# Local attention and a squared-ReLU layer: the first block as two groups of 256 tokens, a hand-fixed issue order, weights converted 1024 columns at a time, s r^2 kept in PSUM

## The chip, the cores and the metric

The kernel runs on one core of one Trainium2 chip. TensorE (PE) multiplies matrices and writes PSUM; VectorE (DVE), ScalarE (ACT) and GpSimd (POOL) do the elementwise work; SyncE (SP) issues the DMAs that bring data from HBM to SBUF. PEld is TensorE's loading of weights, which runs beside its matmuls. The metric is the device time of one execution in microseconds; lower is better. A profiled execution has a span, from its first to its last instruction, and a time, which is a little longer.

## The reference, cut to what matters

```python
# q, k, v: (8 batch, 8 heads, 576 positions, 64), float32; chunks of 64 positions
scores = 1/8 * q_c @ k_c^T                    # inside one chunk only
attn = exp(scores - max) / (sum + 1e-9)
x = (attn @ v_c), heads side by side          # 4608 tokens x 512
h = x @ w_in                                  # w_in: 512 x 2048, given in float64
g = s * relu(h)**2 + b                        # s, b: one number each
out = g @ w_out                               # w_out: 2048 x 512, given in float64
```

## The kernel before

**Blocks.** 4608 tokens are nine blocks of 512. For each block the layer runs over 16 slices j of 128 hidden columns. `up(j)` makes h for the slice: 12 matmuls into one bank of PSUM (`ps_h`, two buffers), because every float32 operand is carried as a high and a low part (fp32r) and three of the four products are summed, over four pieces of 128 rows. Then ScalarE takes the ReLU into `r` (L176), VectorE makes s r^2 in place in `r` (L177), ScalarE adds b and rounds to the high part `gh` (L179), VectorE makes the low part `gl` (L180). `down(j)` adds the slice's product to four accumulators (`ps_o`, L193, 12 matmuls); it runs two slices behind `up`. `store` copies the accumulators to SBUF (L199) and sends them off (L200).

**Attention** of the next block is laid between these steps. In the steady blocks a group has 256 tokens, two groups to a block: `s_scores` (64 matmuls of 64x64, L115, then maximum, subtraction, exponential, sum, normalisation, L118 to L128), `s_pt` (8 transposes L136, copies L137), `s_pv` (64 matmuls L143, then `split` into `xh` and `xl`, L57 and L58). The first block has no block before it and is done in four groups of 128 tokens, before the layer starts.

**Weights** come as float64, two 32-bit words to a number, and stay in SBUF after the first block. There are 32 pieces of 128x512, two for each j: (j, 0) for `up`, (j, 1) for `down`. A piece is loaded into `raw` (L66, 512 KB), and `narrow` and `split` turn it into high and low float32: ScalarE scales both words (L75, L76), VectorE shifts and joins bits (L78, L79), GpSimd adds the tail (L81), ScalarE copies the high part (L57), VectorE subtracts for the low part (L58). Each of these works on 512 columns. `next_weights` does one step of this between two steps of the layer, all through the first block.

**Order.** The code gives the instructions in an order of dependence and priority; a scheduler of the framework, which works with estimated durations, sets the order on each engine's queue from it. In a few places `issue_after` keeps an instruction behind another. All DMAs go through the SP queue, s and b as well, third and fourth in it.

**Buffers.** `raw` has four buffers of 4 KB a partition, for weights and for the queries and keys of later blocks; `rawv` two; the attention tiles `p`, `m`, `z`, `pT` one each; `ps_a`, two banks, one; `ps_o` two of two banks.

Of the kernel before, what the change touches and what calls it, by code (L numbers as in the profile page):

```python
# [8 lines left out]
F32 = mybir.dt.float32  # L9
# [9 lines left out]
def local_attention_then_squared_relu_mlp(ctx: ExitStack, tc, qkv, w, s, b, out):  # L19
# [6 lines left out]
    DFF = NJ * P  # L26
# [3 lines left out]
    LAG = 2  # L30
    assert NTB % 4 == 0
# [4 lines left out]
    tmp = ctx.enter_context(tc.tile_pool(name="tmp", bufs=1))  # L36
# [18 lines left out]

    def split(src, hi, lo):
        nc.scalar.copy(out=hi, in_=src)  # L57
        return nc.vector.tensor_tensor(out=lo, in0=src, in1=hi.bitcast(F32), op=ALU.subtract)  # L58
# [5 lines left out]
    def load_weights(j, which):  # L64
        t = raw.tile([P, DM, 2], F32, name="raw").bitcast(U32)
        nc.sync.dma_start(out=t, in_=w[j, which])  # L66
        if j not in weights:
            weights[j] = slot(F32R)
        return t, weights[j][:, 2 * which, :], weights[j][:, 2 * which + 1, :]

    def narrow(words, hi, lo, *after):
        w_lo, w_hi = words[:, :, 0], words[:, :, 1]
        f = tmp.tile([P, DM], F32, name="f", bufs=2)
        u, i, tail = f.bitcast(U32), f.bitcast(I32), w_lo.bitcast(I32)
        nc.scalar.activation(out=f, in_=w_hi.bitcast(F32), func=AF.Copy, scale=2.0 ** -112)  # L75
        nc.scalar.activation(out=tail, in_=w_lo, func=AF.Copy, scale=2.0 ** -29)  # L76
        with tc.issue_after(after[0]) if after else nullcontext():
            nc.vector.tensor_scalar(out=u, in0=u, scalar1=3, scalar2=None, op0=ALU.logical_shift_left)  # L78
        nc.vector.scalar_tensor_tensor(out=u, in0=w_hi, scalar=0x80000000, in1=u,  # L79
                                       op0=ALU.bitwise_and, op1=ALU.bitwise_or)  # L80
        nc.gpsimd.tensor_tensor(out=i, in0=i, in1=tail, op=ALU.add)  # L81
        return f, hi, lo

    def attention_steps(tb, n, xh, xl, col, bank):
        st = {}
        G = n * NHP

        def s_load():
            st["qk"], st["v"] = [], []
            for i in range(n):
                if tb < 4:
                    t = slot(F32)
                    qk, vt = t[:, 0:2, :], t[:, 2, :]
                else:
                    qk, vt = raw.tile([P, 2, DM], F32, name="raw"), rawv.tile([P, DM], F32, name="v")
                nc.sync.dma_start(out=qk, in_=qkv[tb + i, :, 0:2, :])
                nc.sync.dma_start(out=vt, in_=qkv[tb + i, :, 2, :])  # L100
                st["qk"].append(qk.rearrange("p i (h t) -> p i h t", h=H))
                st["v"].append(vt.rearrange("p (h d) -> p h d", h=H))

        def quarters():
            for i in range(n):
# [5 lines left out]
        def s_scores():  # L111
            ps = bank(0)[:, :, 0:G * CH].rearrange("p c (g k) -> p c g k", g=G)
            for i, hp, c, h, rows, cols in quarters():
                qk = st["qk"][i]
                nc.tensor.matmul(out=ps[cols, c, i * NHP + hp, :], lhsT=qk[rows, 0, h, :], rhs=qk[rows, 1, h, :],  # L115
                                 start=True, stop=True)
            m = att.tile([P, 2, G], F32, name="m")
            nc.vector.tensor_reduce(out=m, in_=ps, op=ALU.max, axis=AX.X)  # L118
            p = att.tile([P, G, 2, CH], F32, name="p")
            st["sub"] = nc.vector.tensor_tensor(out=p.rearrange("p g c k -> p c g k"), in0=ps,  # L120
                                                in1=m.unsqueeze(3).to_broadcast([P, 2, G, CH]), op=ALU.subtract)
            p3 = p.rearrange("p g c k -> p (g c) k")
            nc.scalar.activation(out=p3, in_=p3, func=AF.Exp, scale=1.0 / float(D) ** 0.5)  # L123
            z = att.tile([P, 2 * G], F32, name="z")
            nc.vector.tensor_reduce(out=z, in_=p3, op=ALU.add, axis=AX.X)  # L125
            nc.vector.tensor_scalar_add(out=z, in0=z, scalar1=1e-9)
            nc.vector.reciprocal(out=z, in_=z)
            st["mult"] = nc.vector.tensor_tensor(out=p3, in0=p3, in1=z.unsqueeze(2).to_broadcast([P, 2 * G, CH]), op=ALU.mult)  # L128
            st["p"] = p.rearrange("p g c k -> p g (c k)")

        def s_pt():
            ps = bank(1)
            pT = att.tile([P, n, NHP * P], F32, name="pT")
            for i in range(n):
                for hp in range(NHP):
                    nc.tensor.transpose(out=ps[:, i, hp * P:(hp + 1) * P], in_=st["p"][:, i * NHP + hp, :], identity=ident)  # L136
# [12 lines left out]

        return (s_load, s_scores, s_pt, s_pv), st  # L150

    def block_steps(tb0, n, bank):
        xh = xp.tile([P, NHP, 4 * P], F32R, name="xh")
        xl = xp.tile([P, NHP, 4 * P], F32R, name="xl")
        return xh, xl, [attention_steps(tb0 + i, n, xh, xl, i * P, bank) for i in range(0, 4, n)]
# [140 lines left out]
```

## Time and profile before

| | us |
|---|---|
| runs of the kernel, median (lowest to highest of 3) | 911.28 (910.11 to 911.66) |
| the profiled execution, time | 909.67 |
| the same, span | 907.9 |
| busy in it: TensorE | 863.3 |
| VectorE | 403.8 |
| ScalarE | 323.3 |
| GpSimd | 50.6 |

The page says how long each engine was busy in the span, and when. An average over the span hides that the first block is a different thing from the other eight: only there are weights loaded and converted. GpSimd's whole work lies in it. So the profile is read by stretches: for each, the busy time of every engine, the granted clock and what the DMA moved. In the order of time a line has start, length, engine, line of the code, operation, result <- operands, and, in brackets, how long the engine stood before it and for what. In the groups by line the columns after the count are busy us, mean ns of one, and idle us before them with what ended it.

### The profile page before, as it was taken

What the parts mean: (1) busy time and instruction counts of PE and PEld (TensorE: products, weight loads), DVE (VectorE), ACT (ScalarE), POOL (GpSimd) and SP (SyncE); (2) the same over time, 40 slices, a digit from 0 to 9 for tenths busy, and PEclk for the clock granted to TensorE, in tenths of its full rate; (3) what the DMA queues carried; (4) which work ended last, traced back from release to release, by engine and by line L of the source; (5) the groups of instructions that cost most, each with busy time, mean ns of one, the idle gap of its engine ahead of it and who ended that gap; (6) DMA issues with size and microseconds to landing.
All of it is one profiled execution on the core that took longest, in us unless ns stands there. A gap on an engine that the chain in (4) does not pass through costs nothing.

```text
span 907.9 us, 13635 instructions
## 1 busy us (share of the span) xinstructions
PE 863.3 (95%) x5904; PEld 705.9 (78%) x5904; DVE 403.8 (44%) x544; ACT 323.3 (36%) x517; POOL 50.6 (6%) x38
## 2 busy tenths in 40 slices
PE   3499969999999999999999999999999999999997
PEld 2377757888888888888888888888888888888886
DVE  4789895534253434242434334432543254423221
ACT  3576665333242323322333333233333232323222
POOL 0334342000000000000000000000000000000000
PEclk9999979999999999999999999999999999999999
DMA  6454543210020102010201020101020100001001
GB/s 255 123 176 134 197 137 130 81 52 19 24 94 24 47 24 94 24 47 24 94 24 47 24 94 16 55 24 56 39 70 24 44 5 24 1 0 47 1 1 46
DMA packets 20508, 55.40 MB, mean 61 GB/s; under 512 B 2528, under 2 KB 2528, under 8 KB 20448
## 3 DMA queue, kind: packets, MB, share of 16 engines
q1 hardware_dynamic: 20448, 54.54, 17.5%
q8 instruction: 46, 0.75, 0.4%
q14 instruction: 14, 0.11, 0.0%
HBM read 45.09 MB, written 9.44 MB: 60 GB/s over the span
## 4 chain that ended last, share of the span: by engine, by line
PE 83%; DVE 1%; ACT 1%; DMA 0%; issue 0%; ACTq 0%
PE ps_o L193 39%; PE ps_h L173 39%; PE ps_a L143 2%; PE ps_a L115 2%; PE ps_a L136 1%; DMA raw<-in_w_dram 0%; DVE wp L58 0%; DVE g L180 0%; DVE r L177 0%; DVE f L79 0%; ACT f L75 0%; ACT g L179 0%; DVE xl L58 0%; DVE f L78 0%; ACT f L199 0%
## 5 line engine op out<-in xcount | busy, mean ns | idle before, releaser
L193 PE MATMUL ps_o<-wp,g 128*128 128x512 f32 x1728 | 423.5, 392 | 2.0 <-ACT g L179 1.8
L173 PE MATMUL ps_h<-xh,wp 128*128 128x512 f32 x1152 | 385.0, 394 | 3.4 <-ACT r L176 3.4
L193 PEld LDWEIGHTS ps_o<-wp,g 128*128 128x128 f32 x1728 | 322.5, 188 | 70.7 <-ACT g L179 2.2
L177 DVE SCALAR_TENSOR_TENSOR r<-r,s_col 128x512 f32<-128x512 f32 x144 | 112.5, 781 | 336.2 <-ACT r L176 335.4
L173 PEld LDWEIGHTS ps_h<-xh,wp 128*128 128x128 f32 x1152 | 217.3, 189 | 49.1 <-ACT r L176 4.0
L173 PE MATMUL ps_h<-xl,wp 128*128 128x512 f32 x576 | 226.6, 393 | 0.0
L176 ACT ACTIVATE r<-ps_h 128x512 f32<-128x512 f32 x144 | 85.8, 596 | 265.8 <-PE ps_h L173 257.7
L180 DVE SCALAR_TENSOR_TENSOR g<-r,b_col,g 128x512 fp32r<-128x512 f32 x144 | 113.9, 791 | 92.7 <-ACT g L179 91.9
L179 ACT ACTIVATE g<-r,b_col 128x512 fp32r<-128x512 f32 x144 | 104.2, 723 | 113.3 <-DVE r L177 113.3
L173 PEld LDWEIGHTS ps_h<-xl,wp 128*128 128x128 f32 x576 | 108.9, 189 | 22.6
L81 POOL TENSOR_TENSOR f<-f,raw 128x512 int32<-128x512 int32 x32 | 49.9, 1563 | 96.5 <-DVE f L79 69.7
L58 DVE TENSOR_TENSOR xl<-ps_a,xh 128x512 fp32r<-128x512 f32 x32 | 22.1, 691 | 27.3 <-ACT xh L57 26.5
L137 ACT COPY pT<-ps_a 128x512 f32<-128x512 f32 x36 | 20.8, 577 | 35.8 <-PE ps_a L136 35.3
L136 PE MATMUL ps_a<-ident,p 128*128 128x128 f32 x144 | 24.1, 294 | 8.7 <-DVE p L128 7.4
L123 ACT ACTIVATE p<-p 128x1024 f32<-128x1024 f32 (+1 forms) x20 | 19.5, 974 | 33.6 <-DVE p L120 33.6
L75 ACT ACTIVATE f<-raw 128x512 f32<-128x512 f32 x32 | 21.4, 669 | 27.1 <-DVE wp L58 14.7
L57 ACT CAST xh<-ps_a 128x512 fp32r<-128x512 f32 x32 | 18.8, 587 | 32.7 <-PE ps_a L143 19.8
L199 ACT COPY r<-ps_o 128x512 f32<-128x512 f32 x18 | 10.7, 597 | 54.8 <-PE ps_o L193 54.8
L136 PEld LDWEIGHTS ps_a<-ident,p 128*128 128x128 f32 x144 | 18.9, 151 | 14.4 <-issue 6.8
L58 DVE TENSOR_TENSOR wp<-f,wp 128x512 fp32r<-128x512 f32 x32 | 28.5, 889 | 1.4 <-ACT wp L57 0.9
L125 DVE TENSOR_REDUCE z<-p 128x16 f32<-128x1024 f32 (+1 forms) x20 | 22.2, 1112 | 12.5 <-ACT p L123 12.5
L115 PEld LDWEIGHTS ps_a<-raw 64*64 64x64 f32 x1024 | 17.2, 137 | 11.0 <-issue 9.4
(28 smaller groups left out, 247.7 us busy)
## 6 DMA issues: line engine op xcount, KB each, us to landing
raw<-in_w_dram SPq DMA_DIRECT2D x32, 512.0 KB, 3.6
raw<-in_qkv_dram SPq DMA_DIRECT2D x32, 512.0 KB, 4.2
v<-in_qkv_dram SPq DMA_DIRECT2D x32, 256.0 KB, 3.6
out_dram<-r SPq DMA_DIRECT2D x18, 256.0 KB, 2.3
out_dram<-f SPq DMA_DIRECT2D x18, 256.0 KB, 2.6
wp<-in_qkv_dram SPq DMA_DIRECT2D x4, 512.0 KB, 8.0
wp<-in_qkv_dram SPq DMA_DIRECT2D x4, 256.0 KB, 8.0
s_col<-in_s_dram SPq DMA_DIRECT2D x1, 0.5 KB, 4.1
```

Source lines behind the costliest of these rows:

```text
L58: return nc.vector.tensor_tensor(out=lo, in0=src, in1=hi.bitcast(F32), op=ALU.subtract)
L75: nc.scalar.activation(out=f, in_=w_hi.bitcast(F32), func=AF.Copy, scale=2.0 ** -112)
L81: nc.gpsimd.tensor_tensor(out=i, in0=i, in1=tail, op=ALU.add)
L115: nc.tensor.matmul(out=ps[cols, c, i * NHP + hp, :], lhsT=qk[rows, 0, h, :], rhs=qk[rows, 1, h, :], start=True, stop=True)
L125: nc.vector.tensor_reduce(out=z, in_=p3, op=ALU.add, axis=AX.X)
L136: nc.tensor.transpose(out=ps[:, i, hp * P:(hp + 1) * P], in_=st["p"][:, i * NHP + hp, :], identity=ident)
L173: nc.tensor.matmul(out=ps, lhsT=w[:, c, :], rhs=x[:, c, :], start=(c == 0 and i == 0), stop=(c == NHP - 1 and i == 2))
L176: nc.scalar.activation(out=r, in_=ps, func=AF.Relu)
L177: nc.vector.scalar_tensor_tensor(out=r, in0=r, scalar=s_col, in1=r, op0=ALU.mult, op1=ALU.mult)
L179: nc.scalar.activation(out=gh, in_=r, func=AF.Identity, bias=b_col)
L180: nc.vector.scalar_tensor_tensor(out=gl, in0=r, scalar=b_col, in1=gh.bitcast(F32), op0=ALU.add, op1=ALU.subtract)
L193: nc.tensor.matmul(out=acc[t], lhsT=x[:, ts], rhs=w, start=(j == 0 and i == 0), stop=(j == NJ - 1 and i == 2))
```

## The change

The scheduler is switched off (`manual_schedule`): every engine's queue now holds its instructions in the order in which the code gives them. The order is written out.

- Attention is a class with a method for each step. The first block is done in two groups of 256 tokens, like the others, with its own order. The first matmuls of the layer, `up(0)` and `up(1)`, are each cut in two by tokens (`first`, `second`), the first half ahead of the second group's last steps.
- Weights are converted two pieces at a time, as a `Pair`: one load buffer of 8 KB, and each operation on 1024 columns. Pair k holds piece (k+1, 0) and piece (k-1, 1); the first has (0, 0) and (1, 0) and is done in halves of 512. `raw` has three buffers of 8 KB, `rawv` one, of twice the size.
- `square` takes the ReLU into `r` but writes s r^2 back over h in PSUM, and `bias` reads it there. So the `ps_h` bank is held until `bias` is done.
- s and b are loaded through ScalarE's queue.
- In the loop the steps of attention have fixed places in units of half a slice (`plan`). Loads of the next block's queries, keys and values stand in the block's own first slice.
- `store` uses the `f` buffers alone, two rows of tokens in each.

```diff
-    raw = ctx.enter_context(tc.tile_pool(name="raw", bufs=4))
-    rawv = ctx.enter_context(tc.tile_pool(name="rawv", bufs=2))
+    raw = ctx.enter_context(tc.tile_pool(name="raw", bufs=3))
+    rawv = ctx.enter_context(tc.tile_pool(name="rawv", bufs=1))
...
+    ctx.enter_context(tc.manual_schedule())
...
+    nc.scalar.dma_start(out=s_col, in_=s.unsqueeze(0).to_broadcast([P, 1]))
+    nc.scalar.dma_start(out=b_col, in_=b.unsqueeze(0).to_broadcast([P, 1]))
...
+    pairs = [((0, 0), (1, 0))] + [((k + LAG - 1, 0), (k - 1, 1)) for k in range(1, NJ - 1)] + [((NJ - 2, 1), (NJ - 1, 1))]
...
+        def scale(self, which=(0, 1)):
+            f, low, high, _, _ = self.views(which)
+            nc.scalar.activation(out=f, in_=high.bitcast(F32), func=AF.Copy, scale=2.0 ** -112)
+            nc.scalar.activation(out=low.bitcast(I32), in_=low, func=AF.Copy, scale=2.0 ** -29)
+
+        def bits(self, which=(0, 1)):
+            f, low, high, _, _ = self.views(which)
+            u, i = f.bitcast(U32), f.bitcast(I32)
             nc.vector.tensor_scalar(out=u, in0=u, scalar1=3, scalar2=None, op0=ALU.logical_shift_left)
...
+            nc.vector.scalar_tensor_tensor(out=u, in0=high, scalar=0x80000000, in1=u,
+                                           op0=ALU.bitwise_and, op1=ALU.bitwise_or)
+            nc.gpsimd.tensor_tensor(out=i, in0=i, in1=low.bitcast(I32), op=ALU.add)
+
+        def hi(self, which=(0, 1)):
+            f, _, _, hi, _ = self.views(which)
+            nc.scalar.copy(out=hi, in_=f)
+
+        def lo(self, which=(0, 1)):
+            f, _, _, hi, lo = self.views(which)
+            nc.vector.tensor_tensor(out=lo, in0=f, in1=hi.bitcast(F32), op=ALU.subtract)
...
+        def square(self, j):
+            ps = self.ps[j]
+            r = tmp.tile([P, 4 * P], F32, name="r")
             nc.scalar.activation(out=r, in_=ps, func=AF.Relu)
-            nc.vector.scalar_tensor_tensor(out=r, in0=r, scalar=s_col, in1=r, op0=ALU.mult, op1=ALU.mult)
+            nc.vector.scalar_tensor_tensor(out=ps, in0=ps, scalar=s_col, in1=r, op0=ALU.mult, op1=ALU.mult)
+
+        def bias(self, j):
+            ps = self.ps.pop(j)
             gh, gl = (gp.tile([P, 4 * P], F32R, name="g") for _ in range(2))
-            nc.scalar.activation(out=gh, in_=r, func=AF.Identity, bias=b_col)
-            nc.vector.scalar_tensor_tensor(out=gl, in0=r, scalar=b_col, in1=gh.bitcast(F32), op0=ALU.add, op1=ALU.subtract)
...
+            nc.scalar.activation(out=gh, in_=ps, func=AF.Identity, bias=b_col)
+            nc.vector.scalar_tensor_tensor(out=gl, in0=ps, scalar=b_col, in1=gh.bitcast(F32), op0=ALU.add, op1=ALU.subtract)
...
+    one.load_qk()
+    pair[0].load((0,))
+    two.load_qk()
+    one.load_v()
+    pair[0].load((1,))
+    two.load_v()
+    pair[1].load()
+    pair[2].load()
+    run(one.scores, one.peak, one.sub, two.scores)
+    pair[0].scale((0,))
+    one.exp()
+    pair[0].bits((0,))
+    run(one.sum, one.norm, one.transposes, two.peak, two.sub)
+    pair[0].hi((0,))
+    pair[0].scale((1,))
+    run(one.copies, one.values, two.exp)
+    pair[0].lo((0,))
+    pair[0].bits((1,))
+    run(one.x_hi, two.sum, two.norm, two.transposes, one.x_lo)
+    layer = Layer(0, x)
+    first, second = slice(0, N * P), slice(N * P, 4 * P)
+    layer.up(0, first)
+    pair[0].hi((1,))
+    run(two.copies, two.values)
+    pair[0].lo((1,))
+    pair[1].scale()
+    pair[1].bits()
+    layer.up(1, first)
+    run(two.x_hi, two.x_lo)
...
+            for a, n in zip(groups, (1, 8)):
+                for at, *fs in ((2 * n - 2, a.load_qk, a.load_v), (2 * n, a.scores), (2 * n + 1, a.peak), (2 * n + 2, a.sub, a.exp),
+                                (2 * n + 3, a.sum), (2 * n + 4, a.norm), (2 * n + 6, a.transposes, a.copies),
+                                (2 * n + 8, a.values, a.x_hi), (2 * n + 9, a.x_lo)):
+                    plan.setdefault(at, []).extend(fs)
         for j in range(NJ + LAG):
...
+            if j < NJ:
+                if tb0 or j > 1:
+                    layer.up(j)
+                else:
+                    layer.up(j, second)
+            run(*plan.get(2 * j, ()))
+            if tb0 == 0:
+                if j + 3 < NJ:
+                    pair[j + 3].load()
+                if j + 2 < NJ:
+                    pair[j + 2].scale()
+                    pair[j + 2].bits()
+                if j + 1 < NJ:
+                    pair[j + 1].hi()
+            if j < NJ:
+                layer.square(j)
+            if tb0 == 0 and j + 1 < NJ:
+                pair[j + 1].lo()
+            if j < NJ:
+                layer.bias(j)
+            if j >= LAG:
+                layer.down(j - LAG)
+            run(*plan.get(2 * j + 1, ()))
+        layer.store()
```

The steps of attention keep their operations; they are now methods that the plan can call one by one: `scores` (64 matmuls), `peak`, `sub`, `exp`, `sum`, `norm` (three small to large operations of VectorE), `transposes`, `copies`, `values`, `x_hi` (ScalarE, two halves), `x_lo` (VectorE, two halves).

More of the change, by code (lines that the diff above doesn't have):

```diff
@@ L1 @@
-from contextlib import ExitStack, nullcontext
+from contextlib import ExitStack
 import concourse.bass as bass
@@ L64, in load_weights @@
[L64 to L82, printed above, removed]
@@ L150, in attention_steps, with scores @@
[L150 to L155, printed above, removed]
-    def steady_bank(stage):
-        return ps_a.tile([P, 2, DM], F32, name="ps_a")
+        def scores(self):
+            self.ps = self.bank(0)[:, :, 0:G * CH].rearrange("p c (g k) -> p c g k", g=G)
+            for i, hp, c, h, rows, cols in self.quarters():
+                qk = self.qk[i]
+                nc.tensor.matmul(out=self.ps[cols, c, i * NHP + hp, :], lhsT=qk[rows, 0, h, :], rhs=qk[rows, 1, h, :],
+                                 start=True, stop=True)
@@ new lines, in transposes, with copies @@
+        def transposes(self):
+            p = self.p.rearrange("p g c k -> p g (c k)")
+            self.ps = self.bank(1)
+            for g in range(G):
+                i, hp = divmod(g, NHP)
+                nc.tensor.transpose(out=self.ps[:, i, hp * P:(hp + 1) * P], in_=p[:, g, :], identity=ident)
+        def copies(self):
+            pT = att.tile([P, N, NHP * P], F32, name="pT")
+            for i in range(N):
+                nc.scalar.copy(out=pT[:, i, :], in_=self.ps[:, i, :])
+            self.pT = pT.rearrange("p i (a t) -> p i a t", a=NHP)
@@ new lines, in values, with halves @@
+        def values(self):
+            self.ps = self.bank(2)[:, :, 0:G * CH].rearrange("p c (g t) -> p c g t", g=G)
+            for i, hp, c, h, rows, cols in self.quarters():
+                nc.tensor.matmul(out=self.ps[cols, c, i * NHP + hp, :], lhsT=self.v[i][rows, h, :],
+                                 rhs=self.pT[rows, i, hp, cols], start=True, stop=True)
+        def halves(self):
+            for c in range(2):
+                hi, lo = (x[:, :, :, c * CH:(c + 1) * CH] for x in self.x)
+                yield self.ps[:, c].rearrange("p (i a) t -> p i a t", i=N), hi, lo
@@ L160, in first_bank, with x_hi, x_lo, block @@
+        def x_hi(self):
+            for ps, hi, lo in self.halves():
+                nc.scalar.copy(out=hi, in_=ps)
+        def x_lo(self):
+            for ps, hi, lo in self.halves():
+                nc.vector.tensor_tensor(out=lo, in0=ps, in1=hi.bitcast(F32), op=ALU.subtract)
+    def block(tb0, bank):
+        x = [xp.tile([P, NHP, 4 * P], F32R, name=n) for n in ("xh", "xl")]
+        return x, [Attention(tb0 + i, x, i * P, bank) for i in range(0, 4, N)]
     def first_bank(stage):
@@ new lines, in store, with run @@
+                nc.scalar.copy(out=o[:, t % 2], in_=self.acc[t])
+                nc.sync.dma_start(out=out[(self.tb0 + t) * P:(self.tb0 + t + 1) * P, :], in_=o[:, t % 2])
+    def run(*steps):
+        for f in steps:
+            f()
+    x, (one, two) = block(0, first_bank)
+    pair = [Pair(k) for k in range(NJ)]
+    one.load_qk()
[7 more added lines that the diff above has]
+    run(one.scores, one.peak, one.sub, two.scores)
```

223 lines of the change are left out of this document (95 added, 128 removed).

## Prediction

> **What bounds the kernel now.** I read the page, then the table by stages, then the order of time. The page gives the span and TensorE's share. In the stage table the columns are stretch, length, then busy time (instructions) of PE, PEld, DVE, ACT and POOL, granted clock, DMA share, GB/s. One steady block of 512 tokens is 94.29 us.
>
> ```profile
> span 907.9 us, 13635 instructions
> PE 863.3 (95%) x5904; PEld 705.9 (78%) x5904; DVE 403.8 (44%) x544; ACT 323.3 (36%) x517; POOL 50.6 (6%) x38
> 60.00:70.00 10.00, 10.00 (x46) 8.29 (x45) 10.00 (x17) 6.88 (x11) 3.47 (x2) 1.00 0.28 99
> 110.00:120.00 10.00, 5.44 (x23) 3.80 (x21) 9.75 (x13) 6.86 (x12) 2.58 (x2) 0.91 0.62 211
> 155.15:249.44 94.29, 94.29 (x657) 77.45 (x657) 36.58 (x48) 29.67 (x46) 0.00 (x0) 1.00 0.13 45
> ```
>
> So from 155 us on TensorE has no idle time and no other engine can shorten the span. All that can be won lies before: 42 us of attention and first weights, then a first block in which VectorE is full (10.00, 9.75) while TensorE has holes. These rows from the order of time and the chain fix the ends (start, length, engine, line).
>
> ```profile
> 42.17 1.22 PE L173 MATMUL ps_h<-xh,wp 128*128 128x512 f32 x2
> 44.90 1.05 PE L173 MATMUL ps_h<-xh,wp 128*128 128x512 f32 x2
> 45.75 0.63 PE L173 MATMUL ps_h<-xl,wp 128*128 128x512 f32 x1
> 154.68 2.72 PE ps_o L193 x12
> 161.48 1.09 PE ps_a L115 x64
> 894.72 8.32 PE L193 MATMUL ps_o<-wp,g 128*128 128x512 f32 x36
> ```
>
> The layers' first matmul runs at 42.17. From 44.90 to 45.75 two of them take 0.85, 0.43 each: the slow start of TensorE after idling. In full run twelve take 2.72 us, one 0.2267; I call twelve a packet. The 64 small matmuls of an attention step take 1.09 then. The 36 last ones end at 894.72 + 8.16 = 902.9. A block without attention is 384 x 0.2267 = 87.0. Counted back, 902.9 - 87.0 - 7 x 94.29 = **155.9** is where the second block in effect begins. I forecast that point for the changed kernel and add what is new in the steady blocks.
>
> **The first block's pace.** In both kernels VectorE and GpSimd use the same SBUF tiles there, and this is what they do to each other:
>
> ```profile
> 97.36 1.62 POOL L81 TENSOR_TENSOR f<-f,raw 128x512 int32<-128x512 int32 x1 [2.22 <-ACT xh L57]
> 97.75 0.68 DVE L58 TENSOR_TENSOR xl<-ps_a,xh 128x512 fp32r<-128x512 f32 x1
> 100.13 1.64 POOL L81 TENSOR_TENSOR f<-f,raw 128x512 int32<-128x512 int32 x1 [1.15 <-ACT r L176]
> 100.51 1.81 DVE L177 SCALAR_TENSOR_TENSOR r<-r,s_col 128x512 f32<-128x512 f32 x1
> L177 DVE SCALAR_TENSOR_TENSOR r<-r,s_col 128x512 f32<-128x512 f32 x85 | 63.3, 744 | 216.9 <-ACT r L176 216.2
> 99.30 0.69 DVE L79 SCALAR_TENSOR_TENSOR f<-raw,f 128x512 uint32<-128x512 uint32 x1
> 99.91 0.69 DVE L58 TENSOR_TENSOR wp<-f,wp 128x512 fp32r<-128x512 f32 x1
> 104.39 0.42 DVE L78 TENSOR_SCALAR f<-f 128x512 uint32<-128x512 uint32 x1
> 104.84 0.69 DVE L79 SCALAR_TENSOR_TENSOR f<-raw,f 128x512 uint32<-128x512 uint32 x1
> 105.77 1.31 POOL L81 TENSOR_TENSOR f<-f,raw 128x512 int32<-128x512 int32 x1 [4.00 <-DVE f L79]
> ```
>
> The subtraction from PSUM runs its usual 0.68 inside a GpSimd add; s r^2, both inputs in SBUF, takes 1.81 and ends 0.55 after the add (744 ns without one). So a VectorE operation with two SBUF inputs stands still until the add is over. With s r^2 in PSUM, `square` and the second half of `bias` have one SBUF input each and should be free of it, like the first of these rows. The subtraction `lo` still has two.
>
> Sizes double. How a doubled operation costs (mean ns):
>
> ```profile
> L120 DVE TENSOR_TENSOR p<-ps_a,m 128x1024 f32<-128x1024 f32 x16 | 19.6, 1223 | 0.5
> L120 DVE TENSOR_TENSOR p<-ps_o,m 128x512 f32<-128x512 f32 x4 | 2.8, 689 | 2.6 <-PE ps_a L136 2.6
> L123 ACT ACTIVATE p<-p 128x1024 f32<-128x1024 f32 x16 | 17.0, 1061 | 28.7 <-DVE p L120 28.7
> L123 ACT ACTIVATE p<-p 128x512 f32<-128x512 f32 x4 | 2.5, 626 | 4.8 <-DVE p L120 4.8
> L75 ACT ACTIVATE f<-raw 128x512 f32<-128x512 f32 x32 | 21.4, 669 | 27.1 <-DVE wp L58 14.7 <-DMA raw<-in_w_dram 12.1
> L57 ACT CAST wp<-f 128x512 fp32r<-128x512 f32 x32 | 19.6, 613 | 4.8 <-POOL f L81 4.7
> L176 ACT ACTIVATE r<-ps_h 128x512 f32<-128x512 f32 x144 | 85.8, 596 | 265.8 <-PE ps_h L173 257.7 <-DMA out_dram<-r 6.9
> L179 ACT ACTIVATE g<-r,b_col 128x512 fp32r<-128x512 f32 x144 | 104.2, 723 | 113.3 <-DVE r L177 113.3
> L127 DVE RECIPROCAL z<-z 128x16 f32<-128x16 f32 x16 | 4.0, 251 | 0.5
> L126 DVE TENSOR_SCALAR z<-z 128x16 f32<-128x16 f32 x16 | 2.7, 170 | 0.2
> ```
>
> So 1024 columns cost VectorE 1.22 (1.14 from start to start: neighbours overlap a little, as 100.51 after 99.91 + 0.69 shows), ScalarE 0.43 more than 512: `scale` 1.10 each, `hi` 1.05. `bits` begins with 0.71 (0.42 and the same slope, 0.27 more). GpSimd at 1024 is not in the trace: between one add (1.31) and two (2.6); I take 2.56, nearest to two, since nothing shows a large fixed part. [...] No row here shows the larger size.
>
> One stage j of the first block on VectorE, in the written order: shift 0.71, or 1.22, 0.13 until GpSimd starts (99.30 + 0.69 to 100.13 is 0.14), add 2.56 with `square` hidden in it, `lo` 1.08 behind the add, the `bias` half 0.66: about **6.3 us**. TensorE needs 2 x 2.72 = 5.44. ScalarE's loop is 2 x 1.10 + 1.05 + 0.60 + square 0.75 + 0.72 + handovers 0.15 = 5.5, so it runs ahead. VectorE sets the pace. Fourteen stages have a pair to convert: 88.2.
>
> Attention of the next block adds, in each of two groups: peak 1.14; sub 1.14, then a stand, because `exp` is queued on ScalarE ahead of the next `scale`, and `bits` waits for that (1.06 + 1.10 + 0.15 = 2.3); sum 1.14; norm 1.58 (the two small rows and a product); x_lo 1.22: 8.5. Two groups: 17. TensorE goes on meanwhile by a packet or two, then waits for the weights and the PSUM bank that VectorE releases at each stage's end. `up(j)` can start when stage j-2 ends and is wanted only by the `relu` of stage j, a stage and 2 us later; it takes 2.7, so some 5 us are in hand, enough for the scores, transposes and products put behind it (1.3, 0.8, 1.3). Queued behind `copies` and `x_hi` on ScalarE are the conversions; 1.2 us each, covered by its lead. The SP queue refills pair j+3 when GpSimd is done with pair j: two stages ahead against some 5 us for 1 MB (3.9 for 512 KB by a row below, 1.3 for the rest), one stage where attention holds a buffer. I cost it nothing; a stage each time, 6 us, if not.
>
> **The head.** Group 1 waits for two loads of 512 KB and group 2 follows in program order:
>
> ```profile
> 4.18 1.14 PE L115 MATMUL ps_o<-wp 64*64 64x64 f32 x32 [4.18 <-DMA wp<-in_qkv_dram]
> 10.16 1.14 PE L115 MATMUL ps_o<-wp 64*64 64x64 f32 x32 [4.84 <-DMA wp<-in_qkv_dram]
> 13.29 1.11 PE L136 MATMUL ps_a<-ident,p 128*128 128x128 f32 x4
> 5.00:6.00 1.00, 0.31 (x12) 0.12 (x7) 0.62 (x1) 0.00 (x0) 0.00 (x0) 1.00 0.02 0
> 9.00:10.00 1.00, 0.00 (x0) 0.00 (x0) 0.00 (x0) 0.00 (x0) 0.00 (x0) 1.00 1.01 404
> ```
>
> From 5 to 6 us nothing moves: s and b, 0.5 KB each, are next in the SP queue there. They go to ScalarE's queue, ahead of its first work; worth 0 to 2 us, I take all. At 404 GB/s the second load lands 1.3 after 4.18; scores done 6.6. Then peak and sub 2.5, exp 1.1, sum 1.2, norm 1.7, eight transposes at 0.28: 15.3. The second group's sub waits for them (p has one buffer): 16.4. `lo` and `bits` of the first pair's halves 1.7, sum and norm 2.9: 21.0. Transposes 2.2, `up(0, first)` 12 x 0.25 (half of the slow 0.43, and a little), values 1.3 (1.09 and a change of shape), `x_hi` 1.2, `scale` 1.1: the first stage starts at **29.9** (27 to 33).
>
> Behind the fourteenth stage TensorE still has `up(15)` and three `down`, which the light last stages cover. The second block then begins at 29.9 + 88.2 + 17 + four packets 10.9 = **146.0**, against 155.9: -9.9. It is less than the head's 12 us and the freed operations promise, because `lo` now always meets the add.
>
> **A new wait.** The next loads of queries and keys are issued behind the last store of the block before, and their scores stand right behind `up(1)`:
>
> ```profile
> 248.80 2.88 PE L193 MATMUL ps_o<-wp,g 128*128 128x512 f32 x12
> 252.46 0.36 SPq L200 DMA_DIRECT2D out_dram<-r  x1
> 252.94 0.36 SPq L200 DMA_DIRECT2D out_dram<-f  x1
> DMA to landing us min/median/max: 3.4/3.9/4.4
> ```
>
> A block's last packet ends at 251.5; its last store is issued 1.4 later, so the two loads go at +1.9 and +2.4 and land at +5.8 and +6.3 by the median of 512 KB loads. TensorE comes to them at +5.44 and, for the second half, about +6.1. That is 0.2 to 0.4, 0.7 by the slowest landing, 1.3 if 1 MB of stores goes first. I take 0.5 in 7 blocks: **+3.5** (0 to 9). Now these loads have the whole block before them and nothing waits.
>
> Elsewhere in the steady blocks the bank of `up` is held through `bias` (0.60 + 0.74 + 0.72 + 0.75, about 3 us), and three other packets, 8.2 us, stand before it is needed: nothing. [...] VectorE writing PSUM is in no row; `square` lies under the add, so -0.1 to +0.5 each changes nothing.
>
> Sum: 909.67 (the profiled execution, 907.9 span and 1.8 around it) - 9.9 + 3.5 = 903.3. The median of the runs is 1.6 higher, so **904.9**; for this case alone 897 to 909.
>
> **Rivals.**
> (a) *The add does not hold `lo`, or is far shorter*: ScalarE's 5.5 paces, 14 x 0.8 = 11 less, 894. For it: `lo` is later if `relu` is. Against: 100.51.
> (b) *The loads are later*, 1.3 a block, +5.6: 910.5, no change that a measurement tells (0.2% is 1.8 us). For it: stores and loads share one queue.
> (c) *Slower: s r^2 is not freed.* `square` still reads r and the column s_col from SBUF; if that pair counts as two inputs, it stands until the add ends, and `lo` behind it: 0.71 + 1.22 + 0.13 + 2.56 + 0.66 + 1.14 + 0.66 = 7.1, so 14 x 0.8 = 11 more, 916. It turns the result from a stage of 6.3 + 6.4/14 = 6.75 on. Against: the row at 97.75, though it has no column operand. That the edit then doesn't do what it seems to is this rival.
>
> **Chances.** Forecast 0.53, (a) 0.17, (b) 0.14, (c) 0.16. Faster by over 0.2%: 0.70; within: 0.14; slower: 0.16. The range takes the forecast's own bounds, most of (a), and (b): 892 to 913.
>
> **What would show it.** The first matmul with 256 columns near 23 us and the first `bits` of 1024 columns for pair 2 near 30; stages of 6.3 with `lo` at about 2 us where it waits and `square` at 0.75; GpSimd at 2.4 to 2.6; ScalarE idle ahead of `exp` twice; TensorE waiting for the loads ahead of the scores in each steady block, which are otherwise 94.3. Wrong if the stage is under 6 or near 7, if the head passes 33, or if steady blocks are over 95.

## The result, and the profile after

| | before | changed |
|---|---|---|
| median, us (lowest to highest of 5) | 911.28 (910.11 to 911.94) | 917.35 (915.14 to 919.23) |
| ratio of the two, 95% interval | | 1.0066 (1.0044 to 1.0087) |
| profiled execution: time, span | 909.67, 907.9 | 915.67, 913.9 |
| second block begins at, us | 155.9 | 153.69 |
| the seven steady blocks together | 660.0 | 667.4 |

The change makes the kernel 0.7% slower. The forecast was 904.9 us, faster, with a range of 892 to 913; the time lies above it. (The changed kernel's runs spread over 4 us, those of before over 2.)

These are the page of the changed kernel, and its table by stages with the columns that were used for before.

```profile
span 913.9 us, 13555 instructions
PE 864.8 (95%) x5928; PEld 708.9 (78%) x5928; DVE 398.9 (44%) x483; ACT 308.3 (34%) x466; POOL 39.5 (4%) x23
```

```profile
110.00:120.00 10.00, 7.95 (x32) 6.45 (x32) 9.86 (x10) 5.25 (x7) 2.66 (x2) 0.83 0.30 105
248.78:345.08 96.30, 94.41 (x657) 77.66 (x657) 36.82 (x48) 28.68 (x46) 0.00 (x0) 1.00 0.12 44
```

The page is nearly that of before, and TensorE is busy 95% as before. The stage table is not: in the first block VectorE is still full (9.86), and a steady block has grown from 94.29 to 96.30 (the one shown; they run from 94.94 to this), of which TensorE works only 94.41. The chain of waits has one row for the last 36 matmuls of each block; its start plus its length is where the next block begins.

```profile
145.52 8.17 PE ps_o L255 x36
240.61 8.17 PE ps_o L255 x36
...
812.97 8.16 PE ps_o L255 x36
900.64 8.17 PE ps_o L255 x36
```

The second block begins at 145.52 + 8.17 = 153.69, only 2.2 us before the 155.9 of the old kernel, where the forecast said 9.9. The seven steady blocks take 812.97 - 145.52 = 667.4, which is 7.4 more than 7 x 94.29. The last block takes 87.67, 0.6 more. In span: -2.2 + 7.4 + 0.6 + 0.1 at the end = 5.9, and 913.9 - 907.9 = 6.0.

**Where a steady block loses it.** This is the order of time at the second block's end (start, length, engine, line, what; in brackets the idle time before it and what ended it; the layer's own matmuls are left out).

```profile
248.06 2.19 SPq L263 DMA_DIRECT2D out_dram<-f  x4
250.35 0.89 SPq L124 DMA_DIRECT2D raw<-in_qkv_dram  x2
251.35 0.86 SPq L134 DMA_DIRECT2D v<-in_qkv_dram  x2
252.25 1.15 SPq L124 DMA_DIRECT2D raw<-in_qkv_dram  x2
254.51 0.69 PE L148 MATMUL ps_a<-raw 64*64 64x64 f32 x32 [0.31 <-DMA raw<-in_qkv_dram]
256.79 0.69 PE L148 MATMUL ps_a<-raw 64*64 64x64 f32 x32 [1.58 <-DMA raw<-in_qkv_dram]
```

SP issues the four stores, then the loads of group 1, its values, and group 2's loads. (Group 2's loads are not written in the first slice but at slice 7; in SP's queue nothing stands between, and they go out at once.) TensorE stands at the scores twice, 0.31 and 1.58 us: 94.41 + 1.89 = 96.30, the whole block. The DMA rows of this stretch (240 to 262) show what is crowded there; columns are count, KB each and median us from issue to landing.

```profile
raw<-in_qkv_dram SPq DMA_DIRECT2D x4, 512.0 KB, 6.5
out_dram<-f SPq DMA_DIRECT2D x4, 256.0 KB, 2.2
v<-in_qkv_dram SPq DMA_DIRECT2D x2, 256.0 KB, 6.2
```

A 512 KB load that landed in 3.9 us now takes 6.5.

**Where the first block loses it.** One stage (j = 0), VectorE and one row each of ScalarE and GpSimd:

```profile
32.80 0.68 DVE L96 TENSOR_SCALAR f<-f 128x1024 uint32<-128x1024 uint32 x1
33.52 1.23 DVE L97 SCALAR_TENSOR_TENSOR f<-raw,f 128x1024 uint32<-128x1024 uint32 x1
34.96 2.40 POOL L99 TENSOR_TENSOR f<-f,raw 128x1024 int32<-128x1024 int32 x1 [2.15 <-ACT wp L103]
35.19 0.76 DVE L237 SCALAR_TENSOR_TENSOR ps_h<-ps_h,s_col,r 128x512 f32<-128x512 f32 x1 [0.45 <-ACT r L236]
35.86 2.60 DVE L107 TENSOR_TENSOR wp<-f,wp 128x1024 fp32r<-128x1024 f32 x1
38.38 0.74 DVE L243 SCALAR_TENSOR_TENSOR g<-ps_h,b_col,g 128x512 fp32r<-128x512 f32 x1
38.54 1.12 ACT L90 ACTIVATE f<-raw 128x1024 f32<-128x1024 f32 x1 [1.86 <-DVE wp L107]
39.69 0.69 DVE L96 TENSOR_SCALAR f<-f 128x1024 uint32<-128x1024 uint32 x1 [0.58 <-ACT f L90]
```

From shift to shift 6.89 us; the forecast had 6.3. The square runs its 0.76 inside the add, as forecast, and `lo` (L107) stands in it for 2.60. What was not foreseen is the last pair of rows. The next `scale` (L90) on ScalarE waits for `lo`, because `lo` is the last reader of the `f` buffer that this `scale` writes; there are two, and a pair holds one from `scale` to `lo`. VectorE then stands 0.58 for `scale`.

### The profile page after: what moved, and what is told of

Its sections match the earlier page's. It is cut to its first block, busy times and chain, and to the rows that moved or that the text cites. A ratio compares the mean times of both kernels' runs of the same rounds, so it can differ in the third digit from the quotient of the medians.

```text
span 913.9 us, 13555 instructions
## 1 busy us (share of the span) xinstructions
PE 864.8 (95%) x5928; PEld 708.9 (78%) x5928; DVE 398.9 (44%) x483; ACT 308.3 (34%) x466; POOL 39.5 (4%) x23
## 4 chain that ended last, share of the span: by engine, by line
PE 79%; DVE 7%; ACT 6%; DMA 5%; issue 2%; SPq 1%; ACTq 0%
PE ps_o L255 40%; PE ps_h L229 34%; DMA raw<-in_qkv_dram 4%; DVE wp L107 3%; PE ps_a L178 2%; PE ps_a L189 2%; PE ps_a L148 1%; ACT f L90 1%; ACT raw L91 1%; ACT wp L103 1%; ACT f L262 1%; DMA wp<-in_qkv_dram 1%; ACT r L236 1%; DVE g L243 1%; DVE z L166 1%
## 5 line engine op out<-in xcount | busy, mean ns | idle before, releaser
L229 PE MATMUL ps_h<-xh,wp 128*128 128x512 f32 (+1 forms) x1168 | 385.4, 393 | 21.0 <-DVE g L243 21.0
L237 DVE SCALAR_TENSOR_TENSOR ps_h<-ps_h,s_col,r 128x512 f32<-128x512 f32 x144 | 109.2, 758 | 381.0 <-ACT r L236 381.0
L229 PE MATMUL ps_h<-xl,wp 128*128 128x512 f32 (+1 forms) x584 | 228.3, 391 | 0.8 <-DVE xl L203 0.8
L243 DVE SCALAR_TENSOR_TENSOR g<-ps_h,b_col,g 128x512 fp32r<-128x512 f32 x144 | 108.0, 750 | 97.7 <-ACT g L242 97.7
L242 ACT ACTIVATE g<-ps_h,b_col 128x512 fp32r<-128x512 f32 x144 | 99.2, 689 | 127.5 <-DVE ps_h L237 127.5
L99 POOL TENSOR_TENSOR f<-f,raw 128x1024 int32<-128x1024 int32 (+1 forms) x17 | 38.8, 2284 | 100.6 <-DVE f L97 72.6
L107 DVE TENSOR_TENSOR wp<-f,wp 128x1024 fp32r<-128x1024 f32 (+1 forms) x17 | 40.4, 2378 | 0.0
L262 ACT COPY f<-ps_o 128x512 f32<-128x512 f32 x36 | 19.4, 590 | 44.2 <-PE ps_o L255 44.2
L90 ACT ACTIVATE f<-raw 128x1024 f32<-128x1024 f32 (+1 forms) x17 | 18.3, 1078 | 24.3 <-DVE wp L107 13.2
L148 PE MATMUL ps_a<-raw 64*64 64x64 f32 x1024 | 20.2, 222 | 6.5 <-DMA raw<-in_qkv_dram 6.4
L171 DVE TENSOR_TENSOR p<-p,z 128x1024 f32<-128x1024 f32 x18 | 22.1, 1225 | 0.6
```

Source lines behind the costliest of these rows:

```text
L90: nc.scalar.activation(out=f, in_=high.bitcast(F32), func=AF.Copy, scale=2.0 ** -112)
L99: nc.gpsimd.tensor_tensor(out=i, in0=i, in1=low.bitcast(I32), op=ALU.add)
L107: nc.vector.tensor_tensor(out=lo, in0=f, in1=hi.bitcast(F32), op=ALU.subtract)
L148: nc.tensor.matmul(out=self.ps[cols, c, i * NHP + hp, :], lhsT=qk[rows, 0, h, :], rhs=qk[rows, 1, h, :], start=True, stop=True)
L229: nc.tensor.matmul(out=self.ps[j][:, cols], lhsT=w[:, c, :], rhs=x[:, c, :], start=(c == 0 and i == 0), stop=(c == NHP - 1 and i == 2))
L237: nc.vector.scalar_tensor_tensor(out=ps, in0=ps, scalar=s_col, in1=r, op0=ALU.mult, op1=ALU.mult)
```

## The experiments

The theory after the result: three things ate the gain, and each is separate from the others. (1) In the steady blocks the scores wait for loads queued behind the stores. (2) In the first block two `f` buffers tie ScalarE to VectorE. (3) In the head s and b, now in a second queue, slow the first loads. The rivals: the steady blocks are longer for another reason (PSUM, issue order); VectorE alone sets the stage; the head is late through its order.

### e1: the loads ahead of the stores

```diff
+        if tb0 + 8 < NTB:
+            ahead = block(tb0 + 8, steady_bank)
+            run(ahead[1][0].load_qk, ahead[1][0].load_v)
         layer.store()
```

The block after uses them and leaves out its own first loads.

> The changed kernel, but the loads of the next block's first group (queries, keys, values) are issued ahead of the block's last stores instead of behind them. Theory (the slowdown is the wait of the scores for these loads in every steady block): the seven steady blocks go from 94.9 to 96.3 us back to 94.3 to 94.5, the first block stays as it is (second block begins at 153.7), so about 6 to 7 us less: 908 to 909 in the profiled execution, ratio to the kernel before about 0.998. Rival (holding s r^2 in PSUM, or the fixed order itself, makes the steady blocks longer): blocks stay at 95 or more and the time within 2 us of the changed kernel's 915.7.

906.54 us, all runs within 0.1; against before 0.9954 (0.9941 to 0.9966). From the chain of waits:

```profile
145.32 8.16 PE ps_o L255 x36
239.44 8.16 PE ps_o L255 x36
...
804.16 8.16 PE ps_o L255 x36
```

Each of the seven steady blocks now takes 94.12, and no wait of the scores for a load is left in them. That is less than the 94.3 to 94.5 expected, and the profiled execution is 9.2 us shorter instead of 6 to 7. Moving four DMA issues ahead of four others gives 10.8 us of the median, and with the wait the spread of the runs goes too. (1) is shown.

### e10: the stores in ScalarE's queue

```diff
-                nc.sync.dma_start(out=out[(self.tb0 + t) * P:...
+                nc.scalar.dma_start(out=out[(self.tb0 + t) * P:...
```

> The changed kernel with the four stores of a block issued through ScalarE's queue instead of SP's; the loads still stand where they stood. Theory A (the loads come late because SP's queue holds them back until the last store is issued, and because 1 MB of stores goes ahead of them): the loads are issued up to 4 us earlier and are no longer behind the stores, the steady blocks fall from 95.0 to 96.3 to below 94.5, time near 907. Theory B (the loads are late because the DMA engines are shared among 1 MB of stores and 2.5 MB of loads that come at once, whatever the queue): an earlier issue helps little, the blocks stay above 94.8, time 912 or more.

908.01 us (907.40 to 908.25), ratio to before 0.9963 (0.9949 to 0.9977); the steady blocks are 94.12 again. But the expectation had the reason half wrong. SP's rows:

```profile
225.26 0.84 SPq L124 DMA_DIRECT2D raw<-in_qkv_dram  x2
275.49 0.80 SPq L134 DMA_DIRECT2D v<-in_qkv_dram  x2
```

With no store in the queue, SP does not issue the loads 4 us earlier but more than 20: between these two rows, over 20 us to either side of the block's end at 247.6, it issues nothing, and the 2.5 MB of loads no longer meet the 1 MB of stores. So it was the stores' place in the queue that held the loads back; how much of the 6.5 us of landing is queue and how much shared DMA engines, this run does not tell, since it removes both. It is 1.5 slower than e1. In the last block, with no scores to fill the time, the first square is late behind four copies and four stores on ScalarE, and TensorE stands; the block is 0.7 longer than in e1. About 1 us more goes after the last matmul, where the copies and the stores now take turns on ScalarE.

```profile
818.84 0.50 PE L229 MATMUL ps_h<-xh,wp 128*128 128x512 f32 x1 [1.05 <-DVE g L243]
```

### e2: a third f buffer

```diff
-                self.f = tmp.tile([P, 2, DM], F32, name="f")
+                self.f = tmp.tile([P, 2, DM], F32, name="f", bufs=3)
-            r = tmp.tile([P, 4 * P], F32, name="r")
+            r = tmp.tile([P, 4 * P], F32, name="r", bufs=1)
```

(The `f` of `store` too, and one `r` less.)

> The changed kernel with three f buffers instead of two (and one r buffer instead of two, to make room). Theory (a stage of the first block is 6.9 us and not 6.3 because scale of pair j+3 waits for the f buffer that the subtraction lo of pair j+1 reads last): stages without attention fall from 6.9 to 6.3, VectorE no longer stands 0.58 ahead of the shift, the second block begins 4 us earlier, 149.7, the time falls by about 4. Rival (ScalarE's own work sets the stage): stages stay at 6.9, no gain.

The second block begins at 141.12 + 8.17 = 149.29, so 4.4 earlier; the seven stands of 0.58 are 4.1. Of the stands one of 0.17 is left, and the stages without attention take 6.25 to 6.5 us as expected, all but the first. (2) is shown. In the first one (7.4) the shift itself takes 1.83; elsewhere it takes 0.69.

```profile
28.92 1.23 DVE L97 SCALAR_TENSOR_TENSOR f<-raw,f 128x1024 uint32<-128x1024 uint32 x1
...
31.43 1.83 DVE L96 TENSOR_SCALAR f<-f 128x1024 uint32<-128x1024 uint32 x1
```

The joining ahead of it ends at 30.15. In the changed kernel the same add starts 0.12 after this joining (30.25 and 30.37) and takes 2.44; by that estimate it runs here to 32.7, and the shift, which ends at 33.26, stands for it. (In e9 a shift of 512 columns takes 1.30 at 31.77, the add there from 30.36 to 32.79.) The shift has a single SBUF input, so two SBUF inputs are not the whole condition for standing. In the kernel before, too, shifts of 0.42 took up to 1.53 where an add ran (68.28, the add from 67.75 to 69.52). A sum over `p` (L166), also with one SBUF input, took its usual 1.22 beside an add that began 0.08 after it (12.96 and 13.04 in the changed kernel).

The time hardly follows: 915.86 (913.17 to 919.31), ratio to before 1.0069 (1.0046 to 1.0091), because the steady blocks, still waiting for loads, take 669.4 in its profile, 2 more than in the changed kernel.

### e3 and e11: s and b later

e3 issues the two small loads on SP's queue behind the third pair's loads, e11 on ScalarE's queue behind the first `bits`.

```diff
-    nc.scalar.dma_start(out=s_col, in_=s.unsqueeze(0).to_broadcast([P, 1]))
-    nc.scalar.dma_start(out=b_col, in_=b.unsqueeze(0).to_broadcast([P, 1]))
...
     pair[2].load()
+    nc.sync.dma_start(out=s_col, in_=s.unsqueeze(0).to_broadcast([P, 1]))
+    nc.sync.dma_start(out=b_col, in_=b.unsqueeze(0).to_broadcast([P, 1]))
```

> The changed kernel with the loads of s and b in the SP queue behind the first weights instead of first in ScalarE's queue. Theory (the 4-byte rows of s and b slow the other loads by half from 2 to 5 us): the first scores start near 4.2 instead of 5.9 and are done near 6.6 instead of 9.3; the first conversion stage begins near 30.1 instead of 32.8; 2 to 3 us less. Rival (the first loads are slow by themselves, because five are in flight): scores still done at 8.5 or later, within 1 us of the changed kernel.

> The changed kernel with s and b loaded through ScalarE's queue, but only behind the first bits step instead of first of all (in e3 they went to SP's queue, behind the third pair). Theory (the small loads halve the rate of the first big ones only while they run beside them): first scores done near 6.9 as in e3, the second block begins 2 to 3 us before 153.7. What e3 left open is whether its later landings in the steady blocks come from s and b standing in SP's queue: then here the steady blocks are as in the changed kernel, 95.0 to 96.3, and the time falls by 2 to 3 us; if any shift of the first block does it, they are again 96 to 98.

First the changed kernel, two stretches of 1 us; the last two numbers are the DMA share and GB/s.

```profile
3.00:4.00 1.00, 0.00 (x0) 0.00 (x0) 0.00 (x0) 0.00 (x0) 0.00 (x0) 1.00 0.61 184
4.00:5.00 1.00, 0.00 (x0) 0.00 (x0) 0.00 (x0) 0.00 (x0) 0.00 (x0) 1.00 0.60 148
```

The same of e3:

```profile
3.00:4.00 1.00, 0.00 (x0) 0.00 (x0) 0.00 (x0) 0.00 (x0) 0.00 (x0) 1.00 0.98 397
4.00:5.00 1.00, 0.60 (x23) 0.60 (x26) 0.00 (x0) 0.00 (x0) 0.00 (x0) 1.00 1.06 430
```

And the first maximum, which waits for the scores, in the changed kernel and in e3:

```profile
9.36 1.23 DVE L153 TENSOR_REDUCE m<-ps_o 128x16 f32<-128x1024 f32 x1 [9.36 <-PE ps_o L148]
```

```profile
6.88 1.22 DVE L151 TENSOR_REDUCE m<-ps_o 128x16 f32<-128x1024 f32 x1 [6.88 <-PE ps_o L146]
```

Beside two loads of 0.5 KB each the first big ones move at 148 to 184 GB/s, without them at 397 to 430. The second block begins at 143.05 + 8.17 = 151.22 in e3 and at 151.13 in e11, 2.5 us earlier in both: (3) is shown. In the changed kernel the two are issued at 0.74 and 1.17 and land 5.5 and 7.1 us later, beside the first big loads. Issued later they do not have that price: in e11 the load of s goes at 10.86, from ScalarE's queue as well, behind four loads of 512 KB (issued from 6.93 to 10.50), and the second block begins no later than in e3. Why they cost so much at the start is open; no run here looks at single packets.

The time is again no measure of it: e3 921.45 (916.78 to 922.20), ratio to before 1.0107 (1.0083 to 1.0131), e11 916.77 (915.52 to 918.93), 1.0065 (1.0045 to 1.0084). The steady blocks take 676.0 in e3 and 671.5 in e11, against 667.4. The 96 to 98 us of a block in e3 don't come from s and b standing in SP's queue alone, since e11 has one of 98.07 without that; its other six take 95.1 to 96.3, like those of the changed kernel. What makes the crowded loads land now earlier and now later stays open; the wait itself is gone in e1.

### e4 and e7: s r^2 in SBUF or PSUM

e4 puts s r^2 of the changed kernel back into `r`. e7 does the PSUM edit alone in the kernel before.

```diff
-            nc.vector.scalar_tensor_tensor(out=ps, in0=ps, scalar=s_col, in1=r, ...
+            nc.vector.scalar_tensor_tensor(out=r, in0=r, scalar=s_col, in1=r, ...
```

(e4; `bias` reads `r`. e7 is the reverse, on L177, L179 and L180 of before.)

> The changed kernel with s r^2 written back to r in SBUF and read there, as before. Theory (a VectorE operation with two SBUF inputs stands until the GpSimd add is over, one with a PSUM input does not): square goes from 0.76 to about 2.5 in the first block, lo falls to 1.2, the stage grows by 0.6 to 7.5, the first block by 6 to 9 us; the steady blocks stay as they are. Rival (the PSUM operand is not what frees square): stage and block unchanged, within 1 us.

> The kernel before, with s r^2 left in PSUM and nothing else changed. Theory (the edit frees square and the bias half from the GpSimd adds): their mean in the first block falls from 1065 and 1107 to about 750 ns, up to 10 us of standing go, of which the subtractions take some back; second block 3 to 8 us earlier than 155.9, steady blocks 94.3: 903 to 908. Rival (the bank held through bias stops TensorE, or the scheduler's order changes): no gain or slower.

e4, a single run: 928.12 us, and its second block begins at 162.15, 8.5 later; stages without attention take 7.2 to 7.9 us. (The other 4 us of the time lie in the steady blocks, 672.1 in all, where TensorE waits 9.2 us for loads, against 6.4 in the changed kernel.) Its stage shows the old stand of the square:

```profile
42.36 2.68 DVE L237 SCALAR_TENSOR_TENSOR r<-r,s_col 128x512 f32<-128x512 f32 x1 [0.52 <-ACT r L236]
44.96 1.21 DVE L107 TENSOR_TENSOR wp<-f,wp 128x1024 fp32r<-128x1024 f32 x1
```

e7: 905.23 us (903.99 to 906.29), ratio to before 0.9936 (0.9922 to 0.9951). Its groups by line in 43 to 153 us (count, busy us, mean ns), then those of before:

```profile
L177 DVE SCALAR_TENSOR_TENSOR ps_h<-ps_h,s_col,r 128x512 f32<-128x512 f32 x16 | 11.9, 745 | 0.6 <-ACT r L176 0.5
L180 DVE SCALAR_TENSOR_TENSOR g<-ps_h,b_col,g 128x512 fp32r<-128x512 f32 x16 | 11.9, 743 | 2.9 <-ACT g L179 2.9
```

```profile
L180 DVE SCALAR_TENSOR_TENSOR g<-r,b_col,g 128x512 fp32r<-128x512 f32 x16 | 17.7, 1107 | 2.3 <-ACT g L179 2.3
L177 DVE SCALAR_TENSOR_TENSOR r<-r,s_col 128x512 f32<-128x512 f32 x16 | 17.0, 1065 | 0.9 <-ACT r L176 0.9
```

These two lose 10.9 us on VectorE. The shifts, joinings and subtractions (L78, L79, L58 to `wp`) take 3.4 of it back, 57.8 to 61.2 us in all; GpSimd's 27 adds fall from a mean of 1591 to 1366 ns, which suggests that the adds had stood for VectorE as well. 5.0 us show in the time (profiled executions of 909.67 and 904.64), all in the first block. The steady blocks stay at 94.28. The scheduler also set another order there (the first maximum of the next block, L118, starts at 55.45 instead of 59.01), so the 5.0 are the edit together with the order that came with it; in e4 the order is fixed and the edit is alone. This one edit, without the rest, gives more than twice what the whole change won in the first block.

### e8 and e9: pieces of 512 columns

The kernel of e1 with each pair converted in two pieces.

```diff
-                    pair[j + 2].scale()
-                    pair[j + 2].bits()
+                    for i in range(2):
+                        pair[j + 2].scale((i,))
+                        pair[j + 2].bits((i,))
```

(`hi` and `lo` too, each as two calls.)

> The changed kernel with loads ahead of the stores (as e1), its pairs converted in two pieces of 512 columns. Theory (each piece has its own fixed cost, about 0.15 us on VectorE an operation, and its own GpSimd add against which the next piece's shift stands): stages grow by 0.5 to 1.5 us, the second block begins at 160 to 174 instead of 153.5. Rival (two smaller pieces overlap better between the engines): 153.5 or earlier.

> The kernel of e1 with each pair converted in two pieces of 512 columns (every operation of the conversion issued twice), as in e8; the clock of that run was 0.801, so its time can't be read. Theory (the size of 1024 pays, because one add of 2.4 us holds lo once and the doubled operations save their fixed part of 0.1 to 0.25 us): each stage becomes longer by 0.5 to 1.5 us, and the second block begins at 160 to 174, against 153.5 in e1; time 913 to 927. Rival (halves let VectorE work on one piece while GpSimd adds the other, so nothing is lost): the second block begins at or before 153.5, time 907 or less.

e8 gave 1593.79 us with TensorE at half to 0.6 of its usual rate in every block (last section), so its time says nothing of the edit. e9 gave 904.44 us (two runs, 904.41 and 904.47), ratio to before 0.9927 (0.9907 to 0.9947). The second block begins at 143.61 + 8.16 = 151.77, 1.7 *earlier* than in e1. The theory fell, the rival held. VectorE's groups in 40 to 150 us, e1 first, then e9 (the last number is idle time before them):

```profile
L107 DVE TENSOR_TENSOR wp<-f,wp 128x1024 fp32r<-128x1024 f32 x14 | 36.6, 2611 | 0.0
L97 DVE SCALAR_TENSOR_TENSOR f<-raw,f 128x1024 uint32<-128x1024 uint32 x13 | 15.9, 1226 | 0.4
L237 DVE SCALAR_TENSOR_TENSOR ps_h<-ps_h,s_col,r 128x512 f32<-128x512 f32 x15 | 11.4, 757 | 5.9 <-ACT r L236 5.9
...
L96 DVE TENSOR_SCALAR f<-f 128x1024 uint32<-128x1024 uint32 x13 | 9.0, 691 | 8.4 <-ACT f L90 8.4
```

```profile
L97 DVE SCALAR_TENSOR_TENSOR f<-raw,f 128x512 uint32<-128x512 uint32 x26 | 31.0, 1192 | 0.9
L107 DVE TENSOR_TENSOR wp<-f,wp 128x512 fp32r<-128x512 f32 x28 | 27.0, 1004 | 0.0
L237 DVE SCALAR_TENSOR_TENSOR ps_h<-ps_h,s_col,r 128x512 f32<-128x512 f32 x15 | 11.3, 755 | 1.3 <-ACT r L236 1.3
...
L96 DVE TENSOR_SCALAR f<-f 128x512 uint32<-128x512 uint32 x25 | 10.6, 425 | 4.1 <-ACT f L90 3.4
```

With halves the joining (L97) stands in an add as well (1.71 at 34.17, the add from 34.03 to 35.33; 0.69 at 33.11, without one) and costs 15.1 more, and the shifts 1.6 more; but `lo` stands 9.6 less, and VectorE's idle time ahead of the shift and the square shrinks by 4.3 and 4.6. Net 1.8 less, as the 1.7. In this order, then, 1024 columns at a time win nothing.

### e5 and e6: the three repairs together, and a better order

e5 is e1, e2 and e3 in one. e6 is e5 with two more moves: `exp` goes behind the `scale` of its stage, and `bias` ahead of `lo`.

```diff
-                                for at, *fs in (... (2 * n + 2, a.sub, a.exp),
+                                for at, *fs in (... (2 * n + 2, a.sub),
...
+                exps[n + 1] = a.exp
...
                     pair[j + 2].scale()
+            if j in exps:
+                exps[j]()
...
+            if j < NJ:
+                layer.bias(j)
             if tb0 == 0 and j + 1 < NJ:
                 pair[j + 1].lo()
-            if j < NJ:
-                layer.bias(j)
```

> The three edits of the runs before in one kernel: loads ahead of the stores, third f buffer, s and b late. Theory (three separate costs): they add up, the second block begins at 146.8 (153.5 - 4.2 - 2.5), the steady blocks stay at 94.1, time 900 and ratio to the kernel before 0.988 to 0.989. Rival (they overlap: what one frees the next takes): 903 or more.

> As e5, and in the written order exp behind the scale of its stage, and the bias half ahead of the subtraction lo. Theory (lo stands for the GpSimd add, and the bias half, which has a PSUM input, can run in that time; exp ahead of scale makes VectorE stand 2.1 us in two stages): stages without attention fall from 6.3 to about 5.65, two stages by another 2.1; the second block begins 11 to 13 us earlier than in e5; time 887 to 890. Rival (ScalarE's loop of 5.5 with attention on top, or the waits for weights, takes over): stages of 6 or more, 893 or more.

e5: 900.25 us (900.21 to 900.29), ratio to before 0.9882 (0.9866 to 0.9899); the second block begins at 138.70 + 8.16 = 146.86, 6.8 before the changed kernel's, where the two repairs alone gave 4.4 and 2.5. The costs are separate and add up.

e6: **888.57 us** (888.40 to 888.71), ratio to before **0.9754 (0.9739 to 0.9768)**; the second block begins at 127.08 + 8.16 = 135.24. It beats both kernels. One of its stages:

```profile
32.44 2.41 POOL L97 TENSOR_TENSOR f<-f,raw 128x1024 int32<-128x1024 int32 x1 [2.06 <-DVE f L95]
32.75 0.76 DVE L235 SCALAR_TENSOR_TENSOR ps_h<-ps_h,s_col,r 128x512 f32<-128x512 f32 x1 [0.45 <-ACT r L234]
34.26 0.75 DVE L241 SCALAR_TENSOR_TENSOR g<-ps_h,b_col,g 128x512 fp32r<-128x512 f32 x1 [0.76 <-ACT g L240]
34.93 1.22 DVE L105 TENSOR_TENSOR wp<-f,wp 128x1024 fp32r<-128x1024 f32 x1
```

Now two operations that the add does not hold, square and the `bias` half, lie beside it, and `lo` comes when it is over: 1.22 instead of 2.60. Of the seven stages without attention four take 5.6 us, as expected (5.65), and three 6.0 to 6.15; in these VectorE stands 0.33 to 0.36 for `scale` again. The two stages with `exp` fall from 10.84 and 10.87 in e5 to 8.19 and 8.01, together 5.5 of the 11.6 us by which the second block begins earlier. Both moves act in them, and no run has one move alone.

## Why the prediction was wrong

**What held.** TensorE bounds the steady blocks, but for the waits for loads, and VectorE paces the first block of the changed kernel: yes. Where VectorE waits for nothing else, its stage is the 6.3 of the forecast (6.25 to 6.5 in e2). The add holds an operation with two SBUF inputs and not one with a PSUM input: yes (2.60 and 0.76; the square 2.68 from SBUF in e4, and 1065 ns down to 745 in e7), so rival (c) falls. That its 916 lies near the measured 917.35 is chance: the time it put on the square was lost elsewhere. The rule is not complete, though, since the shift with its one SBUF input stands too (1.83 instead of 0.69 in e2). GpSimd at 1024 was taken as 2.56, with 2.4 to 2.6 as the sign to look for, of which no row of before shows the lower end; it took 2.37 to 2.45. The stand for `exp` was 2.13 against 2.3. VectorE writing PSUM, which is in no row of before, costs little: s r^2 from and to PSUM takes 745 ns in e7's first block and 759 in the changed kernel from 300 to 800 us, 744 in SBUF before in the same stretch. That the next loads' place behind the last store is a new wait: yes (e1). Two of the signs named for being wrong came, a stage near 7 (6.89) and steady blocks over 95 (six of seven); the head stayed just under its 33 (32.8).

**What failed**, 12.4 us in the profiled execution (903.3 forecast, 915.67):

- *"ScalarE's loop is ... 5.5, so it runs ahead."* The operations' lengths were summed, but not the buffer that bounds how far it can run: `scale` of pair j+3 needs the `f` that `lo` of pair j+1 frees. This is the step that made a stage 6.89 instead of 6.3: seven stands of 0.58, 4.1 us of the 4.4 by which fourteen stages with attention were longer (e2: 4.4).
- *"They go to ScalarE's queue ...; worth 0 to 2 us, I take all."* The sign was wrong. A gap in SP's queue was read as the cost of s and b, and no price was set on running them beside the first loads. First scores done at 9.3 instead of 6.6; with them late, 6.9 (e3, e11). That is 2.7 of the head's 2.9.
- *"I take 0.5 in 7 blocks: +3.5."* The mechanism was right, the size was not: 7.4. The landing was taken from loads that had the DMA engines to themselves (3.9; two of them are issued at 256.44, and from 256 to 257 us the DMA moved 18 GB/s); here 1 MB of stores stands before them and 1.5 MB of loads right behind. Rival (b), 1.3 a block, had the size: 667.4 is 8.6 more than seven of e1's 94.12, 1.2 each. The forecast gave it 0.14 and added it to a first block that was itself too short.
- *"The bank of `up` is held through `bias` ...: nothing."* True where scores lie between (94.12 a block in e1); in the last block, which has none, TensorE stands 0.33 for L243, and the block takes 87.67, 0.6 longer. In e4, which does not hold the bank, it takes 87.04.

Head 2.9, stages 4.4, last packets 0.4, steady blocks 3.9, last block 0.6: 12.2 of the 12.4. All four errors point the same way, and each lies in something that the sum of busy times does not hold: a buffer count, a second queue, a queue's neighbours, a bank with no cover. That 1024 columns at a time pay was the expectation of e8 and e9; e9 shows that they win nothing in this order.

## What to carry to other kernels

When an order is written by hand, follow each buffer from its first writer to its last reader, and ask how many steps the count of buffers lets the other engine run ahead; the sum of its busy times doesn't show that (4.4 us here, e2). In a queue that both loads and stores use, issue the next block's loads ahead of this block's stores (94.12 a block in e1, 94.94 to 96.30 in the changed kernel), and keep small loads away from the first big ones (2.5 us, e3). While GpSimd adds from SBUF, give VectorE what has a PSUM input (the square took 0.76 inside an add), and put subtractions, joinings and shifts from SBUF to SBUF behind it (a subtraction took 2.60 in an add and 1.22 behind it, a shift 1.83 and 0.69, a joining of 512 columns 1.71 and 0.69 in e9): that order, with `exp` out of the way of the next `scale`, took 11.6 us off the first block here (e6). The size of the pieces won nothing in the order of e1 (e9); in that of e6 it was not tried.

## What was not expected of the hardware

- Two loads of 0.5 KB in a second queue, issued with the first loads of the kernel, more than halve the rate of the 512 KB loads beside them: 148 to 184 GB/s instead of 397 to 430 from 3 to 5 us, and the first scores end 2.5 us later. With the load of s issued at 10.86 (e11), the second block begins at 151.13, against 153.69.
- Kernels whose scores wait for crowded loads spread over 3 to 6 us from run to run, e1, e5 and e6 over 0.1 to 0.3. The wait cannot be the only source: the kernel before has no such wait, and its runs spread over 1.8 to 3.4.
- In e8 TensorE is slow in every block, 1593.79 us in all; the same kernel took 904.44 in e9. Two ends of blocks from the chain of waits, and two stretches of the stage table, whose third number from the end is the granted clock:

```profile
202.51 16.88 PE ps_o L255 x36
...
1110.56 13.89 PE ps_o L255 x36
```

```profile
300.00:340.00 40.00, 40.00 (x147) 26.07 (x146) 10.41 (x13) 5.31 (x8) 0.00 (x0) 1.00 0.00 0
...
1200.00:1240.00 40.00, 40.00 (x176) 23.68 (x170) 10.51 (x14) 6.59 (x10) 0.00 (x0) 0.56 0.00 0
```

36 matmuls that take 8.17 us elsewhere take 16.88 while the granted clock reads 1.00, 0.47 each, near the 0.43 that two of them took in the kernel before at 44.90, after idling. Later they take 13.89 (0.56 granted from 1200 to 1240 us). So the granted clock alone does not say how fast TensorE runs, and the length of a known packet has to be looked at beside it. No other run of the study did this; its cause is open.
